# Attention and MLP in one program: shape of the matmuls on the block with the global keys

## The chip, the cores and the metric

The kernel runs on one core of one Trainium2 chip. Its metric is the device time of one execution in microseconds. The time before is 1104.96 us, the median of three runs between 1103.4 and 1105.49.

## The reference

For 8 batches and 8 heads there are 512 local and 32 global queries and keys of 64 numbers each. A global query looks at all 544 keys; a local one at the 32 global keys and at the local keys at most 32 places away. The 544 rows of 512 numbers that come out go through a Fourier transform over both axes, of which the real part is added, then a layer norm and an MLP with 2048 hidden units, which is added as well.

```python
s_ll = scale * np.matmul(q_l, k_l.transpose(0, 1, 3, 2))
mask = np.abs(pos[:, None] - pos[None, :]) <= 32
s_ll = np.where(mask, s_ll, -1000000000.0)
s_lg = scale * np.matmul(q_l, k_g.transpose(0, 1, 3, 2))
out_l = np.matmul(sm(np.concatenate([s_lg, s_ll], axis=-1)), np.concatenate([v_g, v_l], axis=2))
...
u = x + np.real(np.fft.fft(np.fft.fft(x, axis=1), axis=2))
un = (u - mu) / np.sqrt(var + 1e-06)
return u + np.maximum(un @ w_ch1, 0.0) @ w_ch2
```

## The kernel before, in words

Numbers that need more than 11 bits of mantissa are carried as two float16 parts, a high and a low one, and a product is three matmuls: high by high, high by low, low by high. In the first two batches the scores are computed in float32 instead.

**Attention.** Work goes by pairs of heads, 32 of them (p = 4 x batch + pair). A pair has two scores tasks (`scores`, L628), each for two blocks of 128 queries, and four values tasks (`values`, L689), one for each block. In a scores task every block has a global part, the 32 global keys (L645: weights are all 128 queries of one head, 64 rows deep, so two matmuls a term, one a head), and a local part, a window of 128 keys for each half block of 64 queries (L655: 64 rows, 64 queries, four matmuls a term, head and half by head and half). Three terms make 6 and 12 float16 matmuls a block, one term makes 2 and 4 in float32. Both parts write the tile `S`. VectorE masks it and takes the maximum (`masked`, L665, tile `pe`), ScalarE makes the exponentials (`exps`, L674) and their high part (`p_hi`, L677), GpSimd the low part (`p_lo`, L681 and L682) in the tile `ph`, and a transposing DMA (`turn`, L687) turns 768 columns of `ph` into the six blocks of `pl`. For each head the three blocks are:

- block 0: rows 0 to 63 zero, 64 to 95 the low part of the global keys, 96 to 127 their high part,
- block 1: the high part of the 128 local keys of the window, block 2: their low part.

A values task sums, for each head and each half block of queries, block 1 and 2 against the values of the window (L703, three matmuls on 128 rows; the values are in `vN`, or, shifted by half a block, in `vS`, which a DMA copies from `vN`, L600 and L601), then block 0 against the block of `vN` that holds the global values twice, in rows 64 to 95 and 96 to 127: rows 64 to 127 by the high part of the values (L705) and rows 96 to 127 by the low part (L707). The two halves of queries write partitions 0 to 63 and 64 to 127 of the same PSUM bank `bk`, side by side. That makes 20 matmuls a task: 12 on 128 rows, 4 on 64, 4 on 32. VectorE divides by the sum (`norm`, L716 to L718). The global queries have tasks of their own (`g_scores`, L739; `g_values`, L776, with 60 matmuls of 32 columns each; their exponentials go through the transposing DMA of L764 into `plg`).

**Transform and MLP.** The output of a batch goes to HBM and comes back (`x_out`, `d_load`), GpSimd folds it, ScalarE and VectorE split it (`eh`, L922 and L926), TensorE transforms it (`d_first`, L973; `d_second`, L1003). Seventeen chunks of 256 rows then go through the layer norm and the MLP: `f_first` (L1128, 12 matmuls of 256 columns a block of hidden units, tile `ps`) and `f_second` (L1146, 512 columns, tile `acc`).

**Order.** Every step is a task with an engine, a planned duration, its inputs, its buffers and a due time. `Plan.order` simulates the engines and takes, of the tasks that can start first, the one of the lowest class and then the earliest due time; the order that results is fixed in each engine's queue. `BIAS` shifts due times by kind of task and stage. All DMAs are issued from SyncE's queue (SP), in its order. MLP work has late due times and fills TensorE between attention tasks.

Of the kernel before, what the change touches and what calls it, by code (L numbers as in the profile page):

```python
# [20 lines left out]
P = 128  # L21
B, H, SL, SG, D = 8, 8, 512, 32, 64
# [276 lines left out]
class Kern:  # L299
# [328 lines left out]
    def scores(self, i):  # L628
        nc, (p, half) = self.nc, divmod(i, 2)
        s = self.st[p]  # L630
        raw = s["b"] < NRAW
        js = (2 * half, 2 * half + 1)
        s["S", half] = S = self.psa.tile([P, 2, 512], F32, name="S", tag="A", bufs=1)
        if raw:
            q, kw, kg = s["q"], s["kw"], self.g[s["b"]]["n"][:, s["hp"], 64:96]
        else:
            qT, kT, kg = s["qT"], s["kT"], s["kg"]
        for n, j in enumerate(js):
            t = 160 * n
            terms = ((0, 0),) if raw else ((0, 0), (0, 1), (1, 0))  # L640
            for x, (a, c) in enumerate(terms):
                for h in range(2):
                    r = slice(64 * h, 64 * h + 64)
                    w, kgr = (q[r, P * j:P * j + P], kg[r]) if raw else (qT[r, a, j], kg[r, c])
                    nc.tensor.matmul(S[:, h, t:t + 32], w, kgr, start=x == 0, stop=x == len(terms) - 1)  # L645
            for x, (a, c) in enumerate(terms):
                for e in range(2):
                    m = HALVES64[j][e]
# [40 lines left out]
    def values(self, i):  # L689
# [7 lines left out]
        pv = s["pv"]  # L697
        es = [slice(64 * e, 64 * e + 64) for e in range(2)]
        for h in range(2):
# [748 lines left out]
```

## Time and profile before

| what | value |
|---|---|
| median of three runs | 1104.96 us |
| the profiled execution | 1105.87 us, span 1104.1 us |
| TensorE busy | 1041.9 us |
| VectorE, ScalarE, GpSimd busy | 530.0, 550.1, 578.7 us |
| mean granted TensorE clock | 0.937 |
| first MLP matmul (L1128) | at 160.2 us |

All times below are from that execution, in microseconds from the start of its span. On a timeline a row gives the start, the duration of the merged instructions, the engine, the line and the shapes; matmuls are pipelined and their ends are modelled, so what a group costs is read from its start to the start of the next row, not from its duration.

### The profile page before, as it was taken

Reading aid. Unit: us, or ns where it says so; the run is one execution under the profiler, and the core shown is the slowest. Engines: PE = TensorE matmul, PEld = TensorE weight load, DVE = VectorE, ACT = ScalarE, POOL = GpSimd, SP = SyncE. Lnnn points to the kernel's source line nnn. Section 1 sums busy time; section 2 is a strip of 40 time slices with the busy share of each in tenths; the row PEclk is TensorE's granted clock in tenths of the full one; section 3 lists DMA queues with packets and bytes.
Section 4 is the critical chain, followed back from the end, with each engine's and each line's share of the span. In section 5 each row is a group of like instructions: output and inputs, shape, how many; then the busy total and the mean of one; then the engine's idle time right before and its main releaser. Section 6 shows DMA issues by size and latency. Waiting matters only on the chain.

```text
span 1104.1 us, 28491 instructions
## 1 busy us (share of the span) xinstructions
PE 1041.9 (94%) x11411; PEld 704.6 (64%) x11411; DVE 530.0 (48%) x1609; ACT 550.1 (50%) x1234; POOL 578.7 (52%) x976
## 2 busy tenths in 40 slices
PE   3886679999999999999999999999999999999996
PEld 2554457666666666666676666766666666666764
DVE  5877784148443464346536543485444352231111
ACT  6887766857765556664665646544241221111110
POOL 5598774868748475757855685595140620110000
PEclk9655559999999999999999999999999999999998
DMA  9997965346664556484564676423524102011000
GB/s 319 276 243 239 292 141 127 110 117 131 145 163 118 121 129 139 120 191 93 125 133 114 118 175 137 119 70 69 104 52 132 39 23 58 6 52 39 1 20 20
DMA packets 215788, 133.02 MB, mean 120 GB/s; under 512 B 167808, under 2 KB 185312, under 8 KB 215656
## 3 DMA queue, kind: packets, MB, share of 16 engines
q1 hardware_dynamic: 215656, 131.21, 49.2%
q8 instruction: 89, 1.46, 0.6%
q14 instruction: 43, 0.35, 0.1%
HBM read 64.97 MB, written 18.35 MB: 75 GB/s over the span
## 4 chain that ended last, share of the span: by engine, by line
PE 90%; DVE 5%; DMA 2%; issue 1%; ACT 1%; SPq 0%; DVEq 0%; ACTq 0%
PE ps L1128 33%; PE acc L1146 32%; PE bk L703 5%; PE bk L705 3%; PE S L655 3%; PE bk L707 3%; PE S L645 2%; PE psd L1003 1%; PE psd L973 1%; DVE pe L665 1%; DVE ps L413 1%; DMA vf<-in_v 1%; PE pvg L776 1%; PE S L739 1%; DVE mx L408 1%
## 5 line engine op out<-in xcount | busy, mean ns | idle before, releaser
L1128 PE MATMUL ps<-uh,wh 128*128 128x256 f16 x3264 | 385.0, 274 | 0.0
L1146 PE MATMUL acc<-wh,h 128*128 128x512 f16 x1632 | 374.8, 379 | 0.0
L1128 PEld LDWEIGHTS <-wh 128*128 128x128 f16 x3264 | 314.5, 99 | 52.8 <-issue 1.4
L1146 PEld LDWEIGHTS <-h 128*128 128x128 f16 x1632 | 154.6, 98 | 166.4 <-issue 0.2
L1133 ACT ACTIVATE h<-ps 128x512 f16<-128x512 f32 x136 | 81.1, 596 | 320.6 <-PE ps L1128 311.7
L1137 DVE SCALAR_TENSOR_TENSOR h<-ps,h 128x512 f16<-128x512 f32 x136 | 93.7, 689 | 254.1 <-ACT h L1133 253.8
L681 POOL TENSOR_TENSOR ph<-pe,ph 128x256 f16<-128x256 f32 x128 | 88.7, 693 | 54.8 <-ACT ph L677 37.5
L674 ACT ACTIVATE pe<-pe,nm 128x160 f32<-128x160 f32 x256 | 88.0, 415 | 23.5 <-DVE nm L665 23.4
L665 DVE CUSTOM_DVE_ANT_0 pe<-S,msk,z 128x160 f32<-128x160 f32 x192 | 62.3, 380 | 66.2 <-PE S L655 46.4
L703 PE MATMUL bk<-vS,pl 128*64 128x65 f16 x768 | 76.4, 212 | 10.7 <-DMA vS<-vN 10.7
L703 PE MATMUL bk<-vN,pl 128*64 128x65 f16 x768 | 76.4, 211 | 5.5 <-DVE mx L422 2.6
L703 PEld LDWEIGHTS <-pl 128*64 128x64 f16 x1536 | 47.9, 116 | 43.8 <-issue 21.9
L596 POOL TENSOR_TENSOR vN<-vf,vN 128x640 f16<-128x640 f32 x32 | 43.7, 1367 | 44.2 <-ACT vN L592 44.0
L677 ACT ACTIVATE ph<-pe 128x320 f16<-128x320 f32 x128 | 54.9, 457 | 7.6 <-DMA pl<-ph 7.6
L705 PE MATMUL bk<-vN,pl 64*64 64x65 f16 x512 | 57.8, 223 | 0.0
L707 PE MATMUL bk<-vN,pl 32*64 32x65 f16 x512 | 57.5, 221 | 0.0
L1027 POOL TENSOR_TENSOR u<-u,asm 128x257 f32<-128x257 f32 x16 | 12.9, 805 | 80.1 <-DMA u<-xs 46.6
L716 DVE TENSOR_SCALAR dn<-bk,z 128x4 f32<-128x4 f32 x64 | 14.0, 219 | 78.4 <-PE bk L707 78.4
L620 POOL TENSOR_TENSOR qT<-qk,qT 128x512 f16<-128x512 f32 x24 | 27.9, 1162 | 34.2 <-ACT qT L615 34.1
L481 POOL TENSOR_TENSOR wh<-wm,wh 128x512 f16<-128x512 f32 x32 | 36.9, 1157 | 14.4 <-ACT wm L474 13.1
L1151 DVE SCALAR_TENSOR_TENSOR u<-acc,ve,u 128x512 f32<-128x512 f32 x34 | 25.5, 750 | 37.0 <-PE acc L1146 37.0
L682 POOL TENSOR_TENSOR ph<-pe,ph 128x64 f16<-128x64 f32 x128 | 42.7, 333 | 0.0
(214 smaller groups left out, 1555.4 us busy)
## 6 DMA issues: line engine op xcount, KB each, us to landing
qk<-in_qk SPq DMA_DIRECT2D x32, 512.0 KB
vf<-in_v SPq DMA_DIRECT2D x32, 320.0 KB
raw<-in_moe_w_ch SPq DMA_DIRECT2D x17, 512.0 KB
vS<-vN SPq DMA_DIRECT2D x64, 130.0 KB
xs<-x SPq DMA_DIRECT2D x32, 256.0 KB
out<-u SPq DMA_DIRECT2D x16, 512.0 KB
x<-xs SPq DMA_DIRECT2D x24, 256.0 KB
u<-xs SPq DMA_DIRECT2D x24, 256.0 KB
```

Source lines behind the costliest of these rows:

```text
L596: self.nc.gpsimd.tensor_sub(vN[:, :, 1, :, 0:64], self.st[p]["vf"], vN[:, :, 0, :, 0:64])
L665: nc.vector.tensor_tensor_reduce(self.per[(4 * p + j) % 4][:, h], S[:, h, 160 * n:160 * n + 160], self.msk[:, j], z[:, 8:9], 3e38, op0=ALU ...
L674: nc.scalar.activation(pe[:, h], pe[:, h], AF.Exp, bias=nm[:, n, h:h + 1], scale=-1.0)
L677: self.nc.scalar.activation(self.phr[i % NPH][:, :, 96:256], self.per[i % 4], AF.Copy)
L681: self.nc.gpsimd.tensor_sub(ph[:, :, 256:384], pe[:, :, 32:160], ph[:, :, 128:256])
L703: nc.tensor.matmul(pv[r, j % 2, h], pl[:, 3 * h + 1 + a, r], v, start=x == 0, stop=False)
L705: nc.tensor.matmul(pv[r, j % 2, h], pl[64:P, 3 * h, r], vN[64:P, 4, 0, h], start=False, stop=False)
L707: nc.tensor.matmul(pv[r, j % 2, h], pl[96:P, 3 * h, r], vN[96:P, 4, 1, h], start=False, stop=True)
L1128: nc.tensor.matmul(ps[:, q], wt[:, w, c0:c0 + P], uh[:, :, 4 * a + kt, :], start=n == 0, stop=n == 11)
L1133: self.nc.scalar.activation(h[:, 0], self.fps[c, fp], AF.Relu)
L1137: self.nc.vector.scalar_tensor_tensor(h[:, 1], self.fps.pop((c, fp)), 0.0, h[:, 0], op0=ALU.max, op1=ALU.subtract)
L1146: nc.tensor.matmul(self.acc_f[c, j], h[:, a, q, j * P:(j + 1) * P], self.w[1, f][:, w, :], start=f == 0 and a == 0 and w == 0, stop=f == 1 ...
```

## The change

The two lines of `values` on the global block take all 128 rows of it, of `pl` as of `vN`: rows 0 to 63 of `pl` are zero there, and the rows of the low part are now multiplied by both parts of the values. In `scores` the global part is split by half blocks of queries: weights of 64 queries instead of 128, four matmuls a term instead of two, on the same tiles as the local part. The table `BIAS` has other numbers; no planned duration changes.

```diff
-BIAS = {('K', 0): 111, ('w_load', 0): 86, ('W', 0): 59,
...
+BIAS = {('load_consts', 0): -57, ('K', 0): -100, ('w_load', 0): 112, ('W', 0): 81,
...
             for x, (a, c) in enumerate(terms):
-                for h in range(2):
-                    r = slice(64 * h, 64 * h + 64)
-                    w, kgr = (q[r, P * j:P * j + P], kg[r]) if raw else (qT[r, a, j], kg[r, c])
-                    nc.tensor.matmul(S[:, h, t:t + 32], w, kgr, start=x == 0, stop=x == len(terms) - 1)
+                for e in range(2):
+                    for h in range(2):
+                        r = slice(64 * h, 64 * h + 64)
+                        w, kgr = (q[r, P * j + 64 * e:P * j + 64 * e + 64], kg[r]) if raw else (qT[r, a, j, 64 * e:64 * e + 64], kg[r, c])
+                        nc.tensor.matmul(S[64 * e:64 * e + 64, h, t:t + 32], w, kgr, start=x == 0, stop=x == len(terms) - 1)
...
-            for r in es:
-                nc.tensor.matmul(pv[r, j % 2, h], pl[64:P, 3 * h, r], vN[64:P, 4, 0, h], start=False, stop=False)
-            for r in es:
-                nc.tensor.matmul(pv[r, j % 2, h], pl[96:P, 3 * h, r], vN[96:P, 4, 1, h], start=False, stop=True)
+            for c in range(2):
+                for r in es:
+                    nc.tensor.matmul(pv[r, j % 2, h], pl[:, 3 * h, r], vN[:, 4, c, h], start=False, stop=c == 1)
```

One line more in `scores` and one less in `values` shift the numbers: L645 becomes L646, L655 becomes L656, L703 becomes L704, and L705 and L707 together become L707.

The order of instructions before and after is shown at three places. On TensorE, in a values task, the end of one head; `pl` are the transposed exponentials, `vN` and `vS` the values, `bk` the sums. Before:

```order
L703 LDWEIGHTS pl
L703 MATMUL bk<-vS,pl 64x65
L705 LDWEIGHTS pl
L705 MATMUL bk<-vN,pl 64x65
L705 LDWEIGHTS pl
L705 MATMUL bk<-vN,pl 64x65
L707 LDWEIGHTS pl
L707 MATMUL bk<-vN,pl 64x65
```

The same place after:

```order
L704 LDWEIGHTS pl
L704 MATMUL bk<-vS,pl 64x65
L707 LDWEIGHTS pl
L707 MATMUL bk<-vN,pl 64x65
L707 LDWEIGHTS pl
L707 MATMUL bk<-vN,pl 64x65
L707 LDWEIGHTS pl
L707 MATMUL bk<-vN,pl 64x65
```

Nothing has moved here: the same number of loads and matmuls, now with all rows. On TensorE, in a float16 scores task, where the global part of a block ends and the local part begins; `qT` are the queries, `kg` the global keys, `kT` the local ones. Before:

```order
L645 LDWEIGHTS qT
L645 MATMUL S<-kg_68,qT 128x32
L655 LDWEIGHTS qT
L655 MATMUL S<-kT_66,qT 64x128
L655 LDWEIGHTS qT
```

After:

```order
L646 LDWEIGHTS qT
L646 MATMUL S<-kg_68,qT 64x32
L656 LDWEIGHTS qT
L656 MATMUL S<-kT_66,qT 64x128
L656 LDWEIGHTS qT
```

The global part has become 12 loads and matmuls with 64 output partitions where it had 6 with 128, in the same place. On SyncE's queue, ahead of the last transforms of the first batch: `rx` and `raw` are loads of MLP weights, `qk` and `vf` of queries, keys and values, `vS` the shifted copy, `plg` the transposed exponentials of the global queries. Before:

```order
L389 DMA rx<-in_moe_w_ch 128x1024
L389 DMA raw<-in_moe_w_ch 128x1024
L525 DMA qk_97<-in_qk 128x1024
L529 DMA vf_72<-in_v 128x640
L764 DMA_TRANSPOSE plg<-pgr 128x10x128
L389 DMA rx<-in_moe_w_ch 128x1024
L600 DMA vS<-vN 64x1040
L601 DMA vS<-vN 64x1040
```

After:

```order
L389 DMA rx<-in_moe_w_ch 128x1024 x2
L389 DMA raw<-in_moe_w_ch 128x1024
L529 DMA vf_72<-in_v 128x640
L389 DMA rx<-in_moe_w_ch 128x1024
L600 DMA vS<-vN 64x1040
L601 DMA vS<-vN 64x1040
L764 DMA_TRANSPOSE plg<-pgr 128x10x128
L688 DMA_TRANSPOSE pl<-ph 128x6x128
```

The shifted copy has gone from behind the transpose of the global queries to ahead of it, and the load of `qk` stands further up, among the reads of the transform.

## Rows read from the trace of the kernel before

**Rows 1.** The page: the span, the first line of busy times, and two rows of the 40 slices (busy tenths of TensorE, granted clock in tenths).

```profile
span 1104.1 us, 28491 instructions
...
PE 1041.9 (94%) x11411; PEld 704.6 (64%) x11411; DVE 530.0 (48%) x1609; ACT 550.1 (50%) x1234; POOL 578.7 (52%) x976
...
PE   3886679999999999999999999999999999999996
...
PEclk9655559999999999999999999999999999999998
```

**Rows 2.** Busy times by stretch: the stretch, its length, then PE, PEld, DVE, ACT and POOL busy with the count of instructions, the granted clock, the share of the DMA engines and GB/s.

```profile
36.00:93.00 57.00, 47.77 (x603) 32.88 (x603) 41.38 (x150) 49.20 (x112) 48.70 (x64) 0.50 1.04 269
...
160.00:843.00 683.00, 682.97 (x8356) 461.84 (x8354) 334.12 (x1084) 388.29 (x891) 425.98 (x724) 0.99 0.54 123
...
172.00:1090.00 918.00, 917.97 (x10001) 620.30 (x9999) 397.38 (x1200) 422.35 (x951) 453.94 (x777) 1.00 0.42 97
```

**Rows 3.** TensorE's waits: who waited for whom, total, times, longest; the first is the longest of 30 to 160 us, the second the only one from 155 us to the end.

```profile
PE bk L703 <- DMA vS<-vN: 10.7, 1, 10.7
...
PE vm L438 <- DVE xg L786: 0.7, 1, 0.7
```

**Rows 4.** TensorE's timeline around one values task in the middle of the run: start, duration, engine, line, tiles, rows by columns of the weights, shape moved, count.

```profile
543.45 1.48 PE L1128 MATMUL ps<-uh,wh 128*128 128x256 f16 x12
544.86 0.22 PE L703 MATMUL bk<-vN,pl 128*64 128x65 f16 x1
...
544.91 0.20 PE L703 MATMUL bk<-vN,pl 128*64 128x65 f16 x1
...
544.95 0.19 PE L703 MATMUL bk<-vN,pl 128*64 128x65 f16 x1
...
545.07 0.22 PE L705 MATMUL bk<-vN,pl 64*64 64x65 f16 x2
545.22 0.21 PE L707 MATMUL bk<-vN,pl 32*64 32x65 f16 x2
545.37 0.22 PE L703 MATMUL bk<-vN,pl 128*64 128x65 f16 x1
...
545.88 1.48 PE L1128 MATMUL ps<-uh,wh 128*128 128x256 f16 x12
```

**Rows 5.** TensorE's timeline: one float16 scores task, first block and start of the second, and one task of the global values with what follows it.

```profile
542.52 0.24 PE L645 MATMUL S<-kg,qT 64*128 64x32 f16 x6
542.69 0.36 PE L655 MATMUL S<-kT,qT 64*64 64x128 f16 x12
542.98 0.24 PE L645 MATMUL S<-kg,qT 64*128 64x32 f16 x6
...
551.93 0.66 PE L776 MATMUL pvg<-vN,plg 128*32 128x65 f16 x60
552.52 0.24 PE L645 MATMUL S<-kg,qT 64*128 64x32 f16 x6
```

**Rows 6.** Counts: instructions of L703 alone up to 160.25 us and after it (length, PE busy and count, PEld busy and count, clock, DMA); the same of L655 after it; and the group of weight loads of L655 by shape, with count, busy time and mean ns of one.

```profile
0.00:160.25 160.25, 19.57 (x312) 12.66 (x312) 0.61 0.95 254
160.25:1104.10 943.85, 57.96 (x1224) 35.28 (x1224) 0.99 0.42 98
...
160.25:1104.10 943.85, 35.08 (x1152) 19.42 (x1152) 0.99 0.42 98
...
L655 PEld LDWEIGHTS <-qT 64*64 64x64 f16 x1152 | 19.4, 106 | 3.1
```

**Rows 7.** TensorE's timeline at half clock: a float32 scores task (first block and the start of the second), and a values task with what follows it.

```profile
36.10 0.64 PE L645 MATMUL S<-gr,qk 64*128 64x32 f32 x4 [0.66 <-DVE nm L665]
36.67 0.70 PE L655 MATMUL S<-qk 64*64 64x128 f32 x8
37.31 0.64 PE L645 MATMUL S<-gr,qk 64*128 64x32 f32 x4
...
38.51 0.26 PE L703 MATMUL bk<-vN,pl 128*64 128x65 f16 x1
...
38.82 0.26 PE L705 MATMUL bk<-vN,pl 64*64 64x65 f16 x2
39.01 0.26 PE L707 MATMUL bk<-vN,pl 32*64 32x65 f16 x2
...
39.89 0.59 PE L464 MATMUL bk<-vac,part 128*128 128x2 f32 x2
```

**Rows 8.** The chain of waits between 36 and 93 us, its shares by line.

```profile
by line: PE bk L703 15.4%; PE S L655 13.3%; PE S L645 12.3%; PE bk L707 9.5%; PE bk L705 9.4%; PE sga L734 6.7%; DVE pe L665 3.8%; issue 3.2%; PE bk L464 2.7%; PE vm L447 2.7%; DVE ps L413 2.3%; DVE mx L408 2.2%; DVE wm L414 2.1%; PE pvg L7
```

**Rows 9.** Timelines of SyncE's queue, VectorE and TensorE around the last transforms of the first batch; brackets give the idle time before and what ended it.

```profile
110.24 3.43 SPq L764 DMA_TRANSPOSE plg<-pgr  x1
...
114.34 0.47 SPq L600 DMA_DIRECT2D vS<-vN  x1
...
119.83 1.16 DVE L926 SCALAR_TENSOR_TENSOR eh<-x,dsc,eh 128x514 f16<-128x514 f32 x1 [0.64 <-ACT eh L922]
...
127.19 0.30 PE L973 MATMUL psd<-c1r,eh 128*128 128x137 f16 x1 [0.20 <-DVE eh L926]
```

**Rows 10.** ScalarE's waits between 160 and 843 us, the one on a values task: total, times, longest.

```profile
ACT vN L592 <- PE bk L705: 20.4, 16, 3.2
```

More of the change, by code (lines that the diff above doesn't have):

```diff
@@ new lines @@
+BIAS = {('load_consts', 0): -57, ('K', 0): -100, ('w_load', 0): 112, ('W', 0): 81, ('w_abs', 0): -17, ('w_low', 0): 9, ('w_bits', 0): 219, ('w_join', 0): 98, ('w_fold', 0): 3, ('w_top', 0): -37, ('w_spread', 0): -597, ('w_scale', 0): 86, ('W', 1): 7, ('W', 2): 99, ('W', 3): -116, ('w_load', 1): -61, ('W', 4): -6, ('w_abs', 1): 16, ('w_low', 1): 1, ('w_bits', 1): -71, ('w_join', 1): 82, ('W', 5): -96, ('W', 6): 21, ('W', 7): 735, ('w_max', 1): 7, ('w_fold', 1): 21, ('w_top', 1): 121, ('w_spread', 1): 2, ('w_scale', 1): 24, ('w_hi', 0): -113, ('w_lo', 0): -330, ('w_hi', 1): 6, ('w_lo', 1): 12, ('b_load', 0): 156, ('D', 0): 37, ('b_load', 1): 38, ('D', 1): 26, ('b_load', 2): 54, ('D', 2): 225, ('b_sum', 2): -181, ('b_total', 2): -7, ('b_scale', 2): -14, ('b_mul', 2): 72, ('b_hi', 2): -25, ('b_lo', 2): -3, ('b_load', 3): 142, ('D', 3): 14, ('b_sum', 3): -73, ('b_total', 3): -13, ('b_scale', 3): 15, ('b_mul', 3): 88, ('b_hi', 3): -62, ('b_lo', 3): -65, ('load', 0): 25, ('P', 0): 391, ('load_v', 0): 252, ('sums_v', 0): 183, ('P', 1): 292, ('s_total', 0): 110, ('G', 0): 23, ('scales', 0): -66, ('P', 2): 422, ('G', 1): -85, ('load', 1): -294, ('P', 4): -636, ('load_v', 1): 19, ('sums_v', 1): -5, ('s_total', 1): 84, ('G', 2): 45, ('scales', 1): -98, ('P', 6): 183, ('P', 7): -110, ('G', 3): 29, ('load', 2): 7, ('P', 8): -4, ('load_v', 2): -150, ('sums_q', 2): 22, ('sums_k', 2): 9, ('sums_v', 2): -405, ('P', 9): -156, ('s_total', 2): -60, ('G', 4): 281, ('scales0', 2): 59, ('scales', 2): 39, ('P', 10): 47, ('P', 11): -111, ('G', 5): 59, ('load', 3): -96, ('P', 12): -93, ('load_v', 3): -61, ('sums_q', 3): -25, ('sums_k', 3): 358, ('sums_v', 3): -345, ('P', 13): 33, ('s_total', 3): 136, ('G', 6): -114, ('scales0', 3): -65, ('scales', 3): 140, ('P', 14): -70, ('P', 15): -116, ('G', 7): -142, ('v_mul', 0): -16, ('v_hi', 0): 18, ('v_lo', 0): -32, ('v_out', 0): 15, ('scores', 0): 235, ('masked', 0): -45, ('exps', 0): 149, ('p_hi', 0): -57, ('p_lo', 0): -209, ('turn', 0): -5, ('values', 0): -16, ('norm', 0): -2, ('g_scores', 0): 52, ('g_max', 0): 16, ('g_exp', 0): -7, ('g_hi', 0): -104, ('g_lo', 0): 10, ('g_turn', 0): -39, ('g_values', 0): -93, ('g_norm', 0): -57, ('v_mul', 1): 6, ('v_hi', 1): -5, ('v_lo', 1): -129, ('v_out', 1): 317, ('scores', 1): -15, ('masked', 1): 842, ('exps', 1): 14, ('p_hi', 1): -1, ('p_lo', 1): -103, ('turn', 1): 26, ('values', 1): 35, ('norm', 1): -40, ('x_square', 1): 146, ('g_scores', 1): 52, ('g_max', 1): -40, ('g_exp', 1): 112, ('g_hi', 1): -110, ('g_lo', 1): 61, ('g_turn', 1): -642, ('g_values', 1): -236, ('g_norm', 1): -360, ('hi_k', 2): -146, ('lo_k', 2): -192, ('mul_q', 2): -755, ('hi_q', 2): 179, ('halo', 2): -736, ('v_mul', 2): -64, ('v_hi', 2): -3, ('v_lo', 2): 50, ('v_out', 2): -179, ('scores', 2): -15, ('masked', 2): 60, ('exps', 2): 56, ('p_hi', 2): -60, ('p_lo', 2): -80, ('turn', 2): -4, ('values', 2): 14, ('x_square', 2): 73, ('x_out', 2): -9, ('g_max', 2): -980, ('g_exp', 2): -41, ('g_hi', 2): 47, ('g_lo', 2): -15, ('g_turn', 2): 123, ('g_norm', 2): -339, ('mul_k', 3): -47, ('hi_k', 3): -751, ('lo_k', 3): 205, ('mul_q', 3): -12, ('hi_q', 3): -162, ('lo_q', 3): -119, ('v_mul', 3): -701, ('v_hi', 3): 140, ('v_lo', 3): 26, ('v_out', 3): -133, ('scores', 3): 5, ('masked', 3): 46, ('exps', 3): 102, ('p_lo', 3): -40, ('turn', 3): 50, ('values', 3): -1047, ('norm', 3): -3, ('x_square', 3): 237, ('x_out', 3): 12, ('g_scores', 3): 77, ('g_max', 3): 44, ('g_exp', 3): 13, ('g_hi', 3): 16, ('g_lo', 3): -24, ('g_turn', 3): 896, ('g_values', 3): 145, ('g_norm', 3): 29, ('g_out', 0): 132, ('g_square', 0): 54, ('dft_scale', 0): 39, ('d_load', 0): -44, ('d_load2', 0): 106, ('d_odd', 0): -66, ('d_even', 0): 127, ('d_even1', 0): -37, ('d_even2', 0): -100, ('d_even3', 0): -24, ('d_odd2', 0): -1245, ('d_odd3', 0): 17, ('d_tail', 0): -58, ('d_tail2', 0): 442, ('d_hi', 0): 92, ('d_lo', 0): -17, ('d_tail_hi', 0): 25, ('d_first', 0): 87, ('d_z', 0): 320, ('d_z2', 0): -35, ('d_second', 0): 12, ('d_df', 0): -72, ('load_pair', 0): -117, ('d_addp', 0): -497, ('d_addv', 0): -633, ('d_rest', 0): 2, ('g_out', 1): 23, ('d_total', 1): 135, ('dft_scale', 1): -116, ('d_load', 1): 178, ('d_load2', 1): -56, ('d_odd', 1): -39, ('d_even', 1): 13, ('d_even1', 1): -43, ('d_even2', 1): 61, ('d_even3', 1): 131, ('d_odd2', 1): 249, ('d_odd3', 1): -117, ('d_tail', 1): -33, ('d_tail2', 1): -13, ('d_hi', 1): -6, ('d_lo', 1): -94, ('d_tail_hi', 1): -1, ('d_tail_lo', 1): -90, ('d_first', 1): -82, ('d_z', 1): -23, ('d_z2', 1): -20, ('d_second', 1): -452, ('d_as', 1): -20, ('d_df', 1): 27, ('load_pair', 1): -92, ('d_addp', 1): -478, ('d_addv', 1): 5, ('d_rest', 1): 21, ('g_out', 2): 113, ('g_square', 2): 27, ('d_total', 2): 63, ('dft_scale', 2): -137, ('d_load', 2): -119, ('d_load2', 2): -67, ('d_odd', 2): -18, ('d_even', 2): -176, ('d_even1', 2): -19, ('d_even2', 2): 188, ('d_even3', 2): 61, ('d_odd2', 2): -121, ('d_odd3', 2): 38, ('d_tail', 2): 51, ('d_tail2', 2): -15, ('d_hi', 2): 42, ('d_lo', 2): -67, ('d_tail_hi', 2): -9, ('d_tail_lo', 2): -68, ('d_first', 2): 11, ('d_z', 2): 59, ('d_z2', 2): -15, ('d_second', 2): 6, ('d_as', 2): 4, ('d_df', 2): -1238, ('d_addp', 2): -70, ('d_addv', 2): 202, ('d_rest', 2): -36, ('g_out', 3): -466, ('g_square', 3): 203, ('dft_scale', 3): 31, ('d_load', 3): 2, ('d_load2', 3): -62, ('d_odd', 3): 31, ('d_even', 3): -84, ('d_even1', 3): 26, ('d_even2', 3): 78, ('d_even3', 3): 56, ('d_odd2', 3): 198, ('d_tail', 3): 1553, ('d_tail2', 3): -262, ('d_hi', 3): 262, ('d_lo', 3): -778, ('d_tail_hi', 3): -517, ('d_tail_lo', 3): -240, ('d_first', 3): 47, ('d_z', 3): -19, ('d_as', 3): -40, ('d_df', 3): -403, ('load_pair', 3): -41, ('d_addp', 3): 311, ('d_addv', 3): -10, ('d_rest', 3): -25, ('l_load', 0): 19, ('l_stats', 0): -91, ('C', 0): -76, ('l_un', 0): 189, ('l_hi', 0): -10, ('l_lo', 0): 161, ('l_turn', 0): 5, ('l_root', 0): 61, ('C', 1): 5, ('l_stats', 1): -52, ('C', 2): -15, ('l_guess', 1): -41, ('l_un', 1): 11, ('l_lo', 1): -221, ('l_turn', 1): 43, ('l_root', 1): 5, ('l_stats', 2): 63, ('C', 4): 70, ('l_guess', 2): -7, ('l_un', 2): 21, ('l_hi', 2): 2, ('l_lo', 2): 53, ('l_turn', 2): 48, ('l_root', 2): -99, ('C', 5): 16, ('l_stats', 3): 32, ('l_guess', 3): 54, ('l_un', 3): -100, ('l_hi', 3): -137, ('l_lo', 3): 132, ('l_turn', 3): -16, ('l_root', 3): -306}
```

1 line of the change is left out of this document (removed).

## The prediction

> **What bounds the kernel now.** I read the page first: TensorE is busy for 1041.9 of 1104.1 us, and its row of slices stands at 9 from about 155 us on, with the granted clock at 9 tenths or more except in the second to fifth slices [rows 1]. The busy times by stretch say the same more sharply [rows 2]: from 160 to 843 us TensorE is busy for 682.97 of 683 us, while DVE, ACT and POOL stand at 334, 388 and 426 us; from 172 to 1090 us the granted clock is 1.00 (2.4 GHz). The list of TensorE's waits has one wait after 155 us, of 0.7 us [rows 3]. So from the first MLP matmul at 160 us to the end, a microsecond taken off TensorE's own work is a microsecond of the kernel, as long as the others keep up. Ahead of 160 us it is different: TensorE runs at granted clock 0.50 (1.2 GHz) and is busy for 47.8 of 57 us between 36 and 93 us, but ACT and POOL are busy for 49.2 and 48.7 of the same 57 us [rows 2].
>
> **A values task, warm.** The timeline of one task [rows 4] starts at 544.86 and hands over at 545.88: 1.02 us for 20 matmuls. In one head (544.86 to 545.37, 0.51 us) the three pairs on all 128 rows start at .86, .91 and .95, that is 0.05 and 0.04 us apart, and the next row, the 64-row pair, starts 0.12 us after the last of them, not 0.04. The 64-row pair and then the 32-row pair take 0.15 us each (545.07, 545.22, 545.37). What separates a cheap pair from a dear one is the row count that follows: each time the number of rows changes, about 0.11 us go by in which nothing new starts. A task has six such changes (three a head: 128 to 64, 64 to 32, 32 to 128 or to what follows). The change keeps the count of matmuls (1,024 on the two lines before, 1,024 after) and makes all 20 of one shape, so five of the six go and the last stays. New task: a first step of 0.05, eight steps of 0.037 (0.04 read, with the two decimals allowing 0.035 to 0.04), and the last pair's 0.12 to the next shape: 0.05 + 8 x 0.037 + 0.12 = 0.47 us. Saved: 0.55 us. All steps at 0.053 would make the task 0.60 (saved 0.42); steps of 0.030, which is what is left of the 0.21 us of three pairs when one isolated pair of 0.15 is taken off and halved, would make it 0.41 (saved 0.61). I take 0.55, since five pairs in a row are just more of the steps read. Of the 128 tasks, 102 start after 160.25 us (1,224 matmuls of L703 by twelve [rows 6]). **Term: 102 x 0.55 = 56 us, bounds 43 and 62.** All of it is on the path, since TensorE has no idle time there to hide it.
>
> **A scores task, warm.** For one block of queries the global part takes 0.17 us (542.52 to 542.69) and the local part 0.29 us (542.69 to 542.98) [rows 5]; two blocks make 0.93 us (542.52 to 543.45 [rows 4]). The local part is three groups of four tiles; with 0.12 us for the shape change at its end, a group takes (0.29 - 0.12) / 3 = 0.057 us. The change doubles the global matmuls (6 to 12 a block) but gives them the tiles of the local part, so three of the four shape changes of a task go. What a group of four 64x64 tiles with only 32 columns costs, no row shows. From above it is bounded by the same group with 128 columns, 0.057; from below by the present pair, (0.17 - 0.12) / 2 = 0.025. The values of the global queries lie nearest: 60 matmuls of four column tiles in 0.59 us (551.93 to 552.52 [rows 5]), 15 groups of 0.039 us. I take 0.04. New task: 6 x 0.04 + 5 x 0.057 + 0.18 = 0.71 us (the last group carries its 0.12). Saved: 0.22; bounds 0.12 and 0.31. Tasks: 1,152 local matmuls after 160.25 us [rows 6], 24 each, so 48. **Term: 48 x 0.22 = 10.5 us, bounds 5 and 15.**
>
> On this term a rule speaks against the change. The Trainium skill, TensorE: Matmul & The Clock Gate, section "Wait — 56ns, not 53.3ns?", says that start-to-start never drops below about 25 ns however few columns are moved; with four tiles a group would then take 0.10 us, the task 6 x 0.10 + 0.29 + 0.18 = 1.07 us (an estimate from that page), scores would lose 7 us and the sum would be 1051. The row of 60 matmuls in 0.59 us, under 10 ns each, disagrees for tiles that lie side by side [rows 5].
>
> **The front, up to 160 us.** At 1.2 GHz a values task takes 1.38 us (38.51 to 39.89), the three full pairs 0.31 and the 64-row pair 0.19 [rows 7], so a step is (0.31 - 0.19) / 2 = 0.06 and the new task 9 x 0.06 + 0.19 = 0.73 us: 26 tasks [rows 6] x 0.65 = 17 us less work. The float32 scores go the same way (0.57 and 0.64 us a part [rows 7]); four narrower loads in place of two may give back what the missing shape changes save, so I count nothing, with minus 3 to plus 6 us. Little of the 17 us can be had. Between 36 and 93 us values hold 34% of the chain of waits [rows 8], 19.5 us, of which half would go, but ACT and POOL have only 8 us of slack in those 57 us [rows 2]. I take 4 us there. Then TensorE sits idle for 10.7 us until the shifted copy of the values lands [rows 3]; it was issued at 114.34, behind a transpose that held SP's queue from 110.24 for 3.43 us [rows 9]. In the new order that copy goes ahead of the transpose, behind three weight loads, a load of values and nothing else that waits long. What is late next is the transform: its first half needs eh, whose DVE step starts at 119.83 and takes 1.16 us, and its second half waited at 127.19 for eh already [rows 9]. So of the 3.5 us that the copy comes earlier I count 2. The transpose itself now stands behind the copy; its reader is a later matmul group of the global values, and half a microsecond of issue is nothing there. **Term: 6 us, bounds minus 2 and plus 12.** Bound of it: the 8 us of slack plus those 3.5.
>
> Elsewhere the new order swaps neighbours: 26 values tasks and 16 scores tasks still stand ahead of the first MLP matmul, and the share of the MLP behind the last values is unchanged, so I count nothing for it in the loop. Its cover is that TensorE has hardly any wait; if an order were bad, waits would show (first rival).
>
> **Sum.** The profiled execution took 1105.87 us, 0.9 over the median of 1104.96, of which 1.8 lie outside the span. 1105.9 - 56 - 10.5 - 6 = 1033. From the bounds: 1105.9 - 62 - 15 - 12 = 1017 and 1105.9 - 43 - 5 + 2 = 1060.
>
> **The rivals.**
> *Supply becomes the bound.* A faster TensorE asks sooner for the next probabilities and values. ACT waits 16 times, 20.4 us in all, for a values task to free the buffer of values [rows 10]; behind it come POOL's low part and the shifted copy, and all of that stays as long as it was. For: such chains don't shrink with TensorE. Against: after the gain the loop has 683 - 66 = 617 us for POOL's 426, and there is no wait now. If half of the gain in the loop came back, 33 us: 1066.
> *It isn't the row count.* If a pair on the last block cost 0.15 us for another reason (its place at the end of a group of sums, say), 128 rows would leave it there and only scores and front would gain: 1089. Against it is that the third pair of the 128-row sums lies on the same sums and follows in 0.04 us [rows 4].
> *Slower: the loads of the small tiles.* A 64-column load takes 106 ns by itself [rows 6]. Were the twelve loads of a global part to run one behind another, a part would take 1.27 us instead of 0.17, 96 parts would add 106 us, and the time would be 1105.9 - 56 - 6 + 106 = 1150. It decides from 0.65 us more a part (62 / 96). Against: the local part issues twelve such loads and is over in 0.29 us [rows 5]. The Trainium skill has a rule that points this way: TensorEngine Tiling (Array Packing), section "Restrictions", says that column tiling switches the fast weight load off; the rows show that the loads of side-by-side tiles overlap all the same.
> *Slower by the clock.* With TensorE 84% busy from 36 to 93 us the granted clock was 0.50 [rows 2]. If waits came into the loop and took the clock down to 1.2 GHz for a good 145 us of it, all would be lost. It needs the first rival several times over.
>
> **How the numbers follow.** Forecast 0.84, supply 0.10 (1050 to 1075), not the row count 0.03, slower by loads or clock 0.03. I predict 1033 us. The range takes in the bounds and the better part of the supply case: 1015 to 1062. A measurement of this kernel can tell about 0.2%, 2 us, from no change: faster 0.95, same 0.01, slower 0.04.
>
> **What would show it.** In the profile after: values tasks of 0.47 us on the timeline, with no 0.12 us step inside; scores tasks near 0.71; TensorE still without waits between 160 us and the end and the clock at 1.00; the first MLP matmul some 6 us earlier. A values task above 0.6, TensorE's waits for vN, pl or uh adding up to tens of microseconds, or a first MLP matmul later than 160 us would prove a step wrong.

## The result, and the profile after

The changed kernel takes 1027.12 us, the median of four runs between 1026.17 and 1029.36. The kernel before, run beside it, takes 1105.22 us (four runs, 1103.4 to 1105.76). The ratio is 0.9299, with an interval of 0.928 to 0.9318. The profiled execution took 1026.17 us.

The page of the changed kernel, the first two lines of [rows 1]:

```profile
span 1024.3 us, 29886 instructions
...
PE 930.3 (91%) x12115; PEld 640.3 (63%) x12115; DVE 528.6 (52%) x1609; ACT 546.5 (53%) x1234; POOL 577.9 (56%) x976
```

TensorE has 704 matmuls more and 111.6 us less busy time; the other engines have what they had. To see which part of that the end felt, the span is cut at the first MLP matmul (L1128), which starts at 160.2 us before and at 156.5 after. Busy times by stretch, columns as in [rows 2]; before, then after:

```profile
0.00:160.20 160.20, 107.83 (x1296) 73.75 (x1297) 123.38 (x380) 122.83 (x276) 118.27 (x180) 0.61 0.95 254
```

```profile
0.00:156.50 156.50, 75.27 (x1425) 56.84 (x1426) 121.97 (x374) 120.96 (x273) 117.01 (x179) 0.71 0.99 260
156.50:1024.30 867.80, 855.03 (x10693) 583.48 (x10691) 406.67 (x1236) 425.50 (x963) 460.85 (x798) 1.00 0.49 106
```

In the front TensorE has 32.6 us less to do, and the front is 3.7 us shorter. What follows is called the loop here: 867.8 us after against 1104.1 - 160.2 = 943.9 before, 76.1 us less. 3.7 + 76.1 = 79.8 us is the whole difference of the spans.

The values task stands on TensorE's timeline of the changed kernel like this; first a task by itself, then two tasks in a row (columns as in [rows 4]):

```profile
418.23 0.22 PE L704 MATMUL bk<-vN,pl 128*64 128x65 f16 x1
...
418.28 0.20 PE L704 MATMUL bk<-vN,pl 128*64 128x65 f16 x1
...
418.32 0.19 PE L704 MATMUL bk<-vN,pl 128*64 128x65 f16 x1
...
418.35 0.23 PE L707 MATMUL bk<-vN,pl 128*64 128x65 f16 x4
...
418.50 0.23 PE L707 MATMUL bk<-vN,pl 128*64 128x65 f16 x4
418.67 2.79 PE L1128 MATMUL ps<-uh,wh 128*128 128x256 f16 x24
```

```profile
407.63 0.22 PE L704 MATMUL bk<-vN,pl 128*64 128x65 f16 x1
...
408.39 2.79 PE L1128 MATMUL ps<-uh,wh 128*128 128x256 f16 x24
```

One task takes 0.44 us (418.23 to 418.67) where it took 1.02 [rows 4]. The 0.12 us ahead of L707 is gone: from the third pair on 128 rows to the first pair on the global block there are 0.03 us (418.32 to 418.35), and the five pairs from there to the last two take 0.15 (418.35 to 418.50). Only the exit is left, some 0.12 us to the shape of L1128. Two tasks in a row take 0.76 us, 0.12 less than twice 0.44: they share one exit.

The scores task, to be read beside [rows 5]:

```profile
402.33 0.27 PE L646 MATMUL S<-kg,qT 64*64 64x32 f16 x12
...
402.62 0.25 PE L646 MATMUL S<-kg,qT 64*64 64x32 f16 x12
402.71 0.34 PE L656 MATMUL S<-kT,qT 64*64 64x128 f16 x12
402.98 2.76 PE L1146 MATMUL acc<-wh,h 128*128 128x512 f16 x12
```

It takes 0.65 us (402.33 to 402.98) where it took 0.93. Twelve matmuls of the second global part take 0.09 us, less than 8 ns each.

TensorE's waits after: all of the loop's (from 156.5 us on), and then the two longest of the front (up to 156.5 us); columns as in [rows 3]:

```profile
PE acc L1146 <- DVE h L1137: 1.5, 1, 1.5
PE bk L707 <- issue: 0.5, 1, 0.5
PE psd L1005 <- DVE zr L993: 0.4, 1, 0.4
PE psd L1003 <- ACT asm L1010: 0.4, 1, 0.4
PE bk L464 <- DVE x L718: 0.2, 1, 0.2
```

```profile
PE S L646 <- DVE nm L666: 27.4, 9, 7.8
PE bk L704 <- DMA vS<-vN: 11.7, 1, 11.7
```

The loop has 3.0 us of waits in 867.8. In the front the time that TensorE saved has become waiting: 27.4 us for VectorE's `nm` of the scores mask, of which the kernel before has 12.1 in the same stretch, and still 11.7 for the shifted copy.

### The profile page after: what moved, and what is told of

It is laid out like the page before. It is cut to its first block, busy times and chain, and to the rows that moved or that the text cites. A ratio compares the mean times of both kernels' runs of the same rounds, so it can differ in the third digit from the quotient of the medians.

```text
span 1024.3 us, 29886 instructions
## 1 busy us (share of the span) xinstructions
PE 930.3 (91%) x12115; PEld 640.3 (63%) x12115; DVE 528.6 (52%) x1609; ACT 546.5 (53%) x1234; POOL 577.9 (56%) x976
## 4 chain that ended last, share of the span: by engine, by line
PE 80%; DMA 6%; DVE 4%; POOL 3%; ACT 2%; SPq 2%; issue 1%; POOLq 0%; ACTq 0%; DVEq 0%
PE ps L1128 34%; PE acc L1146 34%; PE bk L704 3%; DMA vf<-in_v 2%; PE S L656 2%; PE bk L707 1%; PE S L646 1%; DMA raw<-in_moe_w_ch 1%; PE psd L1003 1%; DMA vS<-vN 1%; DMA pl<-ph 1%; PE S L739 1%; PE S L1003 1%; PE psd L973 1%; PE pvg L776 1%
## 5 line engine op out<-in xcount | busy, mean ns | idle before, releaser
L1128 PE MATMUL ps<-uh,wh 128*128 128x256 f16 x3264 | 383.2, 273 | 0.0
L1128 PEld LDWEIGHTS <-wh 128*128 128x128 f16 x3264 | 313.4, 98 | 52.5 <-issue 1.1
L704 PEld LDWEIGHTS <-pl 128*64 128x64 f16 x1536 | 47.8, 120 | 39.0 <-issue 23.5
L704 PE MATMUL bk<-vS,pl 128*64 128x65 f16 x768 | 56.7, 208 | 11.7 <-DMA vS<-vN 11.7
L704 PE MATMUL bk<-vN,pl 128*64 128x65 f16 x768 | 56.9, 207 | 8.7 <-DVE x L718 8.1
L707 PE MATMUL bk<-vN,pl 128*64 128x65 f16 x1024 | 52.6, 205 | 0.5 <-issue 0.5
L646 PE MATMUL S<-gr,qk 64*64 64x32 f32 x256 | 13.5, 287 | 34.4 <-DVE nm L666 27.4
L707 PEld LDWEIGHTS <-pl 128*64 128x64 f16 x1024 | 42.1, 121 | 0.6 <-issue 0.6
L620 POOL TENSOR_TENSOR qT<-qk,qT 128x512 f16<-128x512 f32 x24 | 27.9, 1165 | 19.0 <-ACT qT L615 18.9
```

The source lines that it names most:

```text
L707: nc.tensor.matmul(pv[r, j % 2, h], pl[:, 3 * h, r], vN[:, 4, c, h], start=False, stop=c == 1)
L1128: nc.tensor.matmul(ps[:, q], wt[:, w, c0:c0 + P], uh[:, :, 4 * a + kt, :], start=n == 0, stop=n == 11)
```

## The experiments

All ratios are against the kernel before on the same chip.

**The parts of the change, one at a time.** The first three kernels take one edit each from the diff above: only the two value lines, only the block of scores, only the table `BIAS`. The fourth is the changed kernel with the table of before:

```diff
-BIAS = {('load_consts', 0): -57, ('K', 0): -100, ('w_load', 0): 112, ('W', 0): 81,
+BIAS = {('K', 0): 111, ('w_load', 0): 86, ('W', 0): 59,
```

Expected of the value lines alone:

> The kernel before with only the two lines of the values on all 128 rows; scores and order as before. Theory, each change of the number of rows or columns on TensorE costs about 0.1 us: of 102 warm tasks the single ones go from 1.02 to 0.44 us and those that come in twos from 2.04 to 0.76, some 62 us, and 0 to 4 in the front: 1040 to 1045 us. Rival, the new order brings the gain: above 1070. Rival, narrow row blocks aren't dear by themselves or by the change but the place at the end of a sum is: about 1105.

Of the scores alone:

> The kernel before with only the global part of the scores in 64x64 tiles; values and order as before. Theory of the change of shape: 48 warm tasks from 0.93 to 0.65 us, 13 us, and up to 4 in the front: 1088 to 1093 us. Rival, the doubled loads and matmuls eat what the shapes give: 1100 to 1110.

Of the order alone:

> The kernel before with the new table of due times alone; all matmuls as before. Theory of the change of shape: the loop has no waits to lose, so only the front can move: 1100 to 1108 us. Rival, the order carries part of the gain: 1095 or less.

Of both edits in the old order:

> Both edits with the old table of due times. Theory of the change of shape: 1026 to 1033 us, within 0.6% of the changed kernel. Rival, without the new order TensorE waits for its inputs: 1040 or more, and the trace shows waits between the first MLP matmul and the end.

| kernel | median us | ratio, interval | first MLP matmul at | loop us |
|---|---|---|---|---|
| before | 1105.22 | 1 | 160.2 | 943.9 |
| value lines only | 1041.96 | 0.944, 0.9419 to 0.9461 | 159.7 | 879.6 |
| scores only | 1093.01 | 0.9908, 0.9892 to 0.9924 | 158.8 | 931.1 |
| order only | 1104.15 | 0.9999, 0.9987 to 1.0012 | 159.3 | 942.9 |
| both, old order | 1029.91 | 0.9333, 0.9307 to 0.9358 | 159.0 | 871.7 |
| changed | 1027.12 | 0.9299, 0.928 to 0.9318 | 156.5 | 867.8 |

(The loop is the span less the start of the first MLP matmul, of the profiled execution.) The value lines take 64.3 us out of the loop and the scores 12.8, 77.1 together; both in one kernel take out 72.2 in the old order and 76.1 in the new one. Alone the order moves nothing that can be measured. With both edits in, its medians lie 3 us apart, but the intervals of the last two rows touch, so whether the new order then gives 3 us or nothing stays open. In the two profiled executions the loop's waits are 5.6 us in the old order and 3.0 in the new one.

**Is it the number of changes, or the narrow matmuls?** In the kernel before, the second head is now summed in the opposite order, so that the 32-row pairs of both heads meet. No matmul is widened; each task has one change of shape less, and two tasks in a row another one between them:

```diff
-        for h in range(2):
...
+        full(0, True, False)
+        part(0, 64, 0, False, False)
+        part(0, 96, 1, False, True)
+        part(1, 96, 1, True, False)
+        part(1, 64, 0, False, False)
+        full(1, False, True)
```

(`full` is the three pairs on 128 rows of one head, `part` one pair on the rows from its second argument on.)

> The kernel before, but the second head of a values task in the opposite order (32 rows, 64 rows, then the three pairs on 128), so that a task has five changes of row count instead of six, and four or five where two tasks stand together. The matmuls and their shapes are those of before, none is widened. Theory of the change of shape at 0.11 us: 102 changes inside the tasks and 33 between tasks go, 15 us, and 1 or 2 in the front: 1087 to 1092 us. Rival, a narrow pair is dear by itself: 1105. Rival, the end of a sum is dear: 1105.

Measured: 1085.02 us, ratio 0.9823 (0.9807 to 0.9838), 20 us less than before. TensorE's timeline of this kernel; the four narrow pairs stand in one merged row under the shape of the first:

```profile
531.07 0.22 PE L703 MATMUL bk<-vN,pl 128*64 128x65 f16 x1
...
531.28 0.54 PE L707 MATMUL bk<-vN,pl 64*64 64x65 f16 x8
531.76 0.22 PE L703 MATMUL bk<-vN,pl 128*64 128x65 f16 x1
...
531.98 1.48 PE L1135 MATMUL ps<-uh,wh 128*128 128x256 f16 x12
```

A task takes 0.91 us, 0.11 less than before. In the loop 36 tasks stand alone and 33 times two stand in a row; two in a row take 1.68 us here, 0.36 less than twice 1.02, which is three changes. 36 x 0.11 + 33 x 0.36 = 15.8 us, and the first MLP matmul comes 3.1 us earlier: 18.9 of the 20. The four narrow pairs take 0.48 us (531.28 to 531.76) where they took 0.60, four times 0.15 [rows 4], with the same rows as before: one of them now costs 0.03, so it is not the rows by themselves that cost. The end of a sum is no better a reason. In the first head the 32-row pair still ends the sum here, and in the changed kernel the first head ends its sums amid five pairs that take 0.15 us together (418.35 to 418.50).

**Fewer changes with rows that stay narrow.** The 32-row pair takes 64 rows, like the pair ahead of it:

```diff
-                nc.tensor.matmul(pv[r, j % 2, h], pl[96:P, 3 * h, r], vN[96:P, 4, 1, h], start=False, stop=True)
+                nc.tensor.matmul(pv[r, j % 2, h], pl[64:P, 3 * h, r], vN[64:P, 4, 1, h], start=False, stop=True)
```

> The kernel before, but the low part's pair of the global block takes 64 rows as the high part's does (rows 64 to 127 in place of 96 to 127), so that a head has two changes of row count instead of three. Theory of the change of shape: 204 changes go, 22 us: 1080 to 1085 us. Rival, a narrow pair is dear by itself, 0.15 us each: 1105.

Measured: 1076.51 us, ratio 0.9749 (0.9732 to 0.9765), 28 us less. Its timeline:

```profile
526.51 0.22 PE L703 MATMUL bk<-vN,pl 128*64 128x65 f16 x1
...
526.73 0.22 PE L705 MATMUL bk<-vN,pl 64*64 64x65 f16 x2
526.78 0.20 PE L707 MATMUL bk<-vN,pl 64*64 64x65 f16 x2
526.91 0.22 PE L703 MATMUL bk<-vN,pl 128*64 128x65 f16 x1
...
527.30 1.48 PE L1128 MATMUL ps<-uh,wh 128*128 128x256 f16 x12
```

The pair of L707, which came 0.15 us after L705 in [rows 4], comes 0.05 after it (526.73 to 526.78), and the 0.13 us stands behind L707 now, where the rows go back to 128. A task takes 0.79 us, so 102 x 0.23 = 23.5 us of the loop, and 3.3 of the front.

**What more matmuls of the same shape cost.** The changed kernel with the pair of the values' low part three times in place of once, four pairs more a task; the sums count that low part three times:

```diff
-            for c in range(2):
+            for y, c in enumerate((0, 1, 1, 1)):
                 for r in es:
-                    nc.tensor.matmul(pv[r, j % 2, h], pl[:, 3 * h, r], vN[:, 4, c, h], start=False, stop=c == 1)
+                    nc.tensor.matmul(pv[r, j % 2, h], pl[:, 3 * h, r], vN[:, 4, c, h], start=False, stop=y == 3)
```

> The changed kernel with the pair of the low part issued three times instead of once, four more pairs a task; the sums count that low part three times. Theory of the change of shape: a pair of unchanged shape costs 0.031 us, 0.125 a task, 13 us for the warm tasks and 0 to 5 in the front: 1040 to 1045 us. Rival, a pair at the end of a sum costs 0.15: 1085 or more.

Measured: 1042.34 us, ratio 0.9435 (0.9421 to 0.9449), 15 us more than the changed kernel, 13.3 of them in the loop. Two tasks in a row on its timeline:

```profile
416.36 0.22 PE L704 MATMUL bk<-vN,pl 128*64 128x65 f16 x1
...
417.37 2.79 PE L1128 MATMUL ps<-uh,wh 128*128 128x256 f16 x24
```

1.01 us against 0.76 for eight pairs more: 0.031 us a pair. 102 x 4 x 0.031 = 12.6 us. 408 pairs more on all rows cost that; the 408 that the change widened had cost 0.15 each.

**Is it the changes in the scores, too?** In the kernel before, the local parts of the two blocks of a task go into a loop of their own behind both global parts. All matmuls are as before, and two of the four changes of a task are gone:

```diff
                     nc.tensor.matmul(S[:, h, t:t + 32], w, kgr, start=x == 0, stop=x == len(terms) - 1)
+        for n, j in enumerate(js):
+            t = 160 * n
             for x, (a, c) in enumerate(terms):
```

> The kernel before, but in a scores task the global parts of both blocks stand first and then both local parts, so that a task has two changes of shape instead of four; weights and matmuls as before. Theory of the change of shape: 96 warm changes of 0.11 us go, 10 us, and 0 to 4 in the front: 1091 to 1096 us. Rival, the load of 128 queries is what is slow in the global part: 1105.

Measured: 1093.0 us, ratio 0.9893 (0.9878 to 0.9908). Its timeline:

```profile
515.42 0.32 PE L645 MATMUL S<-kg,qT 64*128 64x32 f16 x12
515.66 0.53 PE L657 MATMUL S<-kT,qT 64*64 64x128 f16 x24
516.12 1.48 PE L1130 MATMUL ps<-uh,wh 128*128 128x256 f16 x12
```

0.70 us against 0.93: 48 x 0.23 = 11 us, and the loop is 10.9 us shorter. Grouping alone gives most of what the smaller tiles give (13.4 us by the timeline, 48 x 0.28). The change to 64 columns does away with one change of shape more and has twice the matmuls.

**The same edit in a third place.** In the transform one matmul on 64 rows (L1005) stands between matmuls on 128 (L1003). Its two operands are made 128 rows high with zeros below, on top of the changed kernel:

```diff
-    alt = np.zeros((64, NH), np.float16)
+    alt = np.zeros((P, NH), np.float16)
...
-        self.zr = c.tile([64, NK], F16, name="zr")
+        self.zr = c.tile([P, NK], F16, name="zr")
```

(The load of `alt` becomes 128 rows high as well.)

> The changed kernel with the 24 matmuls of L1005 in the transform on 128 rows instead of 64 (64 rows of zeros added to both operands); each stood between matmuls on 128 rows. Theory of the change of shape: two changes less each, 0.2 us, of which 21 lie in the loop: 4.5 us less than the changed kernel, 1021 to 1024 us. Rival, a change of shape costs only where small tiles are involved: 1027, the same.

With it ran the changed kernel once more:

> The changed kernel once more, on the same chip as the run with the wide matmuls: 1027 us, ratio 0.930.

Measured: 1020.3 us (1019.27 to 1021.61), ratio 0.9239 (0.9226 to 0.9251), against 1026.72 and 0.9297 (0.9281 to 0.9313) for the changed kernel beside it: 6.4 us less, and the fastest kernel of this study. TensorE's timeline, in the changed kernel and then in this one:

```profile
813.17 0.34 PE L1003 MATMUL S<-c2r,z 128*128 128x129 f16 x3
813.44 0.23 PE L1005 MATMUL S<-altr,zr 64*128 64x129 f16 x1
813.60 0.35 PE L1003 MATMUL S<-c2r,z 128*128 128x129 f16 x3
813.78 0.51 PE L1003 MATMUL psd<-c2r,z 128*128 128x129 f16 x6
```

```profile
806.97 0.34 PE L1003 MATMUL S<-c2r,z 128*128 128x129 f16 x3
807.14 0.22 PE L1005 MATMUL S<-altr,zr 128*128 128x129 f16 x1
...
807.37 0.51 PE L1003 MATMUL psd<-c2r,z 128*128 128x129 f16 x6
```

0.61 us became 0.40 (two changes of 0.105 each); 21 such places in the loop give 4.4 us. In the profiled executions the loop's waits are 1.4 us shorter (1.3 against 2.7 in the changed kernel beside it) and the first MLP matmul comes 0.4 us earlier (156.0 against 156.4), which makes 6.2 of the 6.4. Whether those 1.8 us come of the edit was not tried.

## Why the prediction was right

**What bounds it: right.** The loop is TensorE's own work. In every kernel above with one edit to the matmuls the loop moved by what the timeline says of its tasks, to within 3 us.

**The values: the mechanism right, the term mis-sized.** Predicted were 102 x 0.55 = 56 us. It is 63 to 64 us: 64.3 in the loop with the value lines alone, and by the timeline 36 x 1.02 + 33 x 2.04 = 104.0 us before against 34 x 0.44 + 34 x 0.76 = 40.8 after (the new order has 34 tasks alone and 34 times two in a row). Two steps of the working were off. Steps inside a run of equal pairs are 0.031 us, not 0.037: 0.05 and 0.04 are only the first two of a run, and the 0.030 of the prediction's other reading was the right one. And the exit was counted for all 102 tasks, while two tasks in a row share it: 34 x 0.12 = 4 us, which could have been read from the order of before, where 33 pairs of tasks stand side by side. The price of one change, 0.116 us ((1.02 - 0.44) / 5), was as predicted (0.11 to 0.12), and the runs with one, two and five changes less a task (0.11, 0.23 and 0.58 us) show that it is the same each time. The rival that the row count isn't the cause falls with the mirrored heads. Nor is it a longer load of weights that fills the gap. One load of the kernel before, from TensorE's timeline of loads:

```profile
545.07 0.11 PEld L705 LDWEIGHTS <-pl 64*64 64x64 f16 x2
```

It starts together with its matmuls, 0.12 us after the last pair on 128 rows (544.95 [rows 4]): in the gap neither a load nor a matmul starts.

The Trainium skill, TensorEngine Tiling (Array Packing), section "Key Properties", says that a change of the tiling mode drains TensorE, without a price. These runs agree that such a change costs time and put it at 0.10 to 0.12 us at granted clock 1.00; that it is the emptying of the array that takes this time, no run here shows.

**The scores: right, a little small.** Predicted 10.5 us, measured 12.8 (scores alone) and 48 x 0.28 = 13.4 by the timeline. The value chosen for a group of four tiles with 32 columns, 0.04, is 0.03 (0.09 / 3). The rival of the slower loads is refuted: no part got slower. The Trainium skill's least distance of about 25 ns from start to start (TensorE: Matmul & The Clock Gate, "Wait — 56ns, not 53.3ns?") is not what tiles side by side show here: twelve matmuls in 0.09 us.

**The front: the direction right, the term too large, its parts wrong.** Predicted 6 us, measured 3.7. It was made of 4 us from TensorE's shorter work between 36 and 93 us and 2 from the shifted copy. Rows of the changed kernel, one from SyncE's queue and two from TensorE, to be read beside [rows 9] and [rows 3]:

```profile
108.00 0.47 SPq L600 DMA_DIRECT2D vS<-vN  x1
```

```profile
116.75 0.26 PE L704 MATMUL bk<-vS,pl 128*64 128x65 f16 x1 [11.68 <-DMA vS<-vN]
...
123.21 0.30 PE L973 MATMUL psd<-c1r,eh 128*128 128x137 f16 x1 [0.37 <-DVE eh L926]
```

The copy is issued 6.3 us earlier, ahead of the transpose as the order said, but takes longer to land, and TensorE is let go at 116.75, 3.7 us before the 120.47 of the kernel before. The second half of the transform follows at 123.21 against 127.19 [rows 9]. TensorE itself arrived at the copy 4.7 us earlier (105.07 against 109.74) and lost that to the wait. So the 4 us were there and did not reach the end: the overlap of that work with the wait for the copy is what the prediction had wrong. That the earlier copy alone gave the 3.7 is not shown, though. With the order alone TensorE is let go at 117.80, and with both edits in the old order at 118.58, but the first MLP matmul comes only 0.9 and 1.2 us earlier; in the two experiments without the new order that removed changes from the values (mirrored heads, 64 rows for both) it comes 3.1 and 3.3 earlier, and with the value lines alone 0.5. What ends the front last in each of them was not tried by a run of its own and stays open; among all kernels that ran, the first MLP matmul lies between 156.0 and 160.2 us.

TensorE's work in the front also fell by more than was counted, 32.6 us where the prediction had 17 for the values. The rest is the float32 scores. One task of the changed kernel, with what follows it, to be read beside [rows 7]:

```profile
39.59 0.44 PE L646 MATMUL S<-gr,qk 64*64 64x32 f32 x8 [0.15 <-DVE nm L666]
...
41.07 1.02 PE L776 MATMUL pvg<-vN,plg 128*32 128x65 f16 x60
```

It takes 1.48 us where it took 2.41 (36.10 to 38.51 [rows 7]), and the 16 such tasks make 15 us. The prediction counted nothing for them, with bounds of minus 3 and plus 6, since narrower loads might give back what the changes save; they gave nothing back. The changes are only a part of this: with grouped scores, which have two changes less, the float32 task takes 2.06 us (35.85 to 37.91 on that kernel's timeline), and what the rest is was not tried. That this slip does not show in the time is luck: the end of the front did not follow TensorE's work.

**The supply: did not become the bound.** 3.0 us of waits in the loop, where half of the gain, 33 us, was the price of that rival. The slower clock did not come either: 1.00 in the loop.

Together: 63.2 + 13.4 + 3.7 = 80.3 us by the timelines, 79.8 by the spans, 72.5 predicted. The forecast of 1033 was 6 us too high: the values gave 7.2 us more than was counted and the scores 2.9 more, the front 2.3 less.

## What to carry to other kernels

On TensorE's timeline read the start of each small matmul against the start of the next, and look where rows or columns of the weights change: a change cost 0.10 to 0.12 us here, as much as three or four pairs of matmuls (96 rows beside 128 were an exception, see below), so equal shapes are worth zero rows, or just an order in which like stands beside like. Count the changes between neighbouring tasks too, not only those inside one. And where another engine or a DMA sets the end of a stretch, as in the front here, even 30% less work on TensorE (107.8 to 75.3 us) moved that end by little.

## What was not expected of the hardware

**A matmul on 96 rows between matmuls on 128 costs no change.** TensorE's timeline of the changed kernel, in the first half of the transform:

```profile
629.11 0.34 PE L973 MATMUL S<-c1r,eh 128*128 128x137 f16 x3
629.29 0.23 PE L975 MATMUL S<-c1tr,ht 96*128 96x137 f16 x1
629.35 0.34 PE L973 MATMUL S<-c1r,eh 128*128 128x137 f16 x3
```

Four matmuls take 0.24 us (629.11 to 629.35), and L975 with its 0.06 is no dearer than the others, while L1005 on 64 rows had 0.1 us on both sides.

**The granted clock shown for the front is not always the pace of TensorE.** Busy times by stretch of two executions of the changed kernel, the one above and the one of the last group of runs:

```profile
100.00:150.00 50.00, 24.12 (x404) 18.14 (x397) 41.44 (x100) 37.38 (x83) 38.40 (x57) 0.50 1.03 241
```

```profile
100.00:150.00 50.00, 24.37 (x409) 18.38 (x407) 41.61 (x100) 37.66 (x84) 39.03 (x57) 1.00 1.02 244
```

By the granted clock, TensorE had 1.2 GHz (0.50) from 100 to 150 us in one and 2.4 GHz (1.00) in the other, at nearly the same busy times. Its timeline in that stretch, in the same two executions:

```profile
123.42 0.55 PE L973 MATMUL psd<-c1r,eh 128*128 128x137 f16 x3
...
123.88 0.55 PE L973 MATMUL psd<-c1r,eh 128*128 128x137 f16 x3
```

```profile
119.92 0.55 PE L973 MATMUL psd<-c1r,eh 128*128 128x137 f16 x3
...
120.38 0.55 PE L973 MATMUL psd<-c1r,eh 128*128 128x137 f16 x3
```

Four matmuls take 0.46 us in both, and 0.24 in the loop (629.11 to 629.35 above). So TensorE went at the slower pace in both fronts, and the 1.00 of the second is not the clock that it had there. Why the profile shows it stays open. The pace is safer read from the starts of matmuls of one shape; what a faster clock would have been worth in the front, no run shows.
